# Sharing out the inverse stage's items in front of and behind a W piece, in an FNet and H3 kernel on one core

## The chip, the core and the metric

The kernel runs on one core of a Trainium2 chip. A core has five engines with an instruction queue each: TensorE (PE, matrix products, its weight loads shown as PEld), VectorE (DVE), ScalarE (ACT), GpSimd (POOL) and SyncE (SP, which here only issues transfers). Transfers issued from SP, ACT and POOL share 16 DMA engines. The metric is the device time of one execution in microseconds; three executions of the kernel before are given, and one more was taken by the profiler.

## The reference, cut to what matters

Four residual layers of 2048 rows by 576 columns follow each other: A, B, A, B. A is a Fourier mixing layer, written as products with cosine and sine matrices. B is a long convolution along the rows, per column, with gates.

```python
def _A_ref(x, dft_seq_re, dft_seq_im, dft_hid_re, dft_hid_im):
    a = jnp.einsum("bsd,ed->bse", x, dft_hid_re)
    b = jnp.einsum("bsd,ed->bse", x, dft_hid_im)
    return jnp.einsum("ts,bse->bte", dft_seq_re, a) - jnp.einsum("ts,bse->bte", dft_seq_im, b)

def _B_ref(q, k, v, shift_k, ssm_k, ssm_D):
    k_shift = ...                      # causal convolution of k with 4 taps
    kv = k_shift * v
    kv_f = rfft(pad(kv)); kf_f = rfft(pad(ssm_k))
    y = irfft(kv_f * kf_f)[:, :S, :] + kv * ssm_D
    return q * y

x = A_x
x = x + _A_ref(_layernorm(x), ...)
x = x + _B_ref(_layernorm(x), B_k, B_v, B_shift_k, B_ssm_k, B_ssm_D)
x = x + _A_ref(_layernorm(x), ...)
x = x + _B_ref(_layernorm(x), B_k, B_v, B_shift_k, B_ssm_k, B_ssm_D)
```

The convolution y depends on k, v and the kernels alone, not on x. It is computed once and used by both B layers.

## The kernel before, in words

Two streams of work share the engines. The first is the **layer** stream, the first A layer. It runs 4 row blocks of 512 times 2 parts (cosine, sine) times 16 slices of 128, which makes 128 steps numbered n, 32 to a row block. A step of the layer loads one 128x512 tile of the sequence matrix (SP), splits it into a high and a low part (`split`: one ACT instruction, one DVE instruction, lines 99 and 100), and multiplies: 12 matmuls into the accumulators s_69 to s_72 and 2 into rm, all 512 columns wide. When both parts of a row block are done, its result U must still be multiplied with the hidden matrices W. This is the work of `hidden`: 8 **W pieces** to a row block, each 27 matmuls of 288 columns into one PSUM bank, which a DVE instruction then adds to the residual (line 289). `finish(pending, 1)` emits one W piece. The pieces of a row block are emitted during the next block: one behind each odd step up to n % 32 = 13, and what is left at step 15 of the block. So the pieces of the last group here stand at n = 97, 99, 101, 103, 105, 107, 109 and 111. This text calls them W97 to W111.

The second stream is the **branch**, the convolution, a generator `br` whose every `next` emits a little and returns a cost. From n = 47 on it has two kinds of item. The first 64 are middle items (forward product, product with the kernel's spectrum, inverse product); each ends in a store to the scratch tensor vd, issued from ACT's queue (line 550). The 32 others are **inverse items** (`i2_products`, line 552): a load of one slice of vd from SP (line 580), a split into `mid` by ACT (line 514) and DVE (line 520), four matmuls of 288 columns into two banks, and for each of the banks an ACT copy (line 514) and a DVE addition (line 561) of 64 partitions, and a store to yb from SP (line 562). Ten inverse items stand between middle items, and 22 behind the last one. Those 22 are the six items E10 to E15, which need the first column half of vd, and then F0 to F15, which need the second half. Every F item reads what all of the last 32 middle items stored, so the first F load waits for the last store.

W pieces, middle products and inverse items take their banks from one ring of three (`bank`, tile name bk), in the order in which they are emitted. An inverse item takes two, a W piece one. Buffers for the stores of middle and inverse items come from one ring of four (`vo`).

What paces the branch is a count. `passed` grows by a step's estimated time whenever the layer yields (about STEP = 3.2 for a step) and by PIECE = 3.6 for a W piece, each in estimated microseconds; `spent` is the branch's cost so far, 3.1 for a middle item and 2.0 for an inverse one. As long as `spent < work * passed / total` (line 816), the next item is emitted. In the kernel before this loop stands behind `finish(pending, 1)` and `passed += PIECE`, so that whatever falls due by the step or by the piece is emitted behind the piece. What the branch emits carries an order edge behind the newest residual addition on DVE (`behind(*added, *evac)`). A scheduler then puts the emitted instructions into the engines' queues, and each engine works its queue off in order.

Of the kernel before, what the change touches and what calls it, by code (L numbers as in the profile page):

```python
# [45 lines left out]
I2_LATE = 6  # L46
I2_COST = 2.0
PIECE = 3.6
STEP = 3.2
KP = 4  # L50
H = 2 * P
# [15 lines left out]
def fnet_h3_kernel(ctx: ExitStack, tc: tile.TileContext, x, c_mat, w_re, w_im, k_pad, v, shift_k,  # L67
# [7 lines left out]
    def mm(ps, lhsT, rhs, first, last, more=False):  # L75
        return nc.tensor.matmul(ps, lhsT, rhs, start=first, stop=last, skip_group_check=more).ins  # L76
# [25 lines left out]
    @contextmanager  # L102
    def behind(*instructions):
        with ExitStack() as stack:
            for i in instructions:
                stack.enter_context(tc.issue_after(i))
            yield
# [11 lines left out]
    def region_b(dt, name):  # L119
        return sb.tile([P, 6 * WIDE], dt, tag="rb", name=name)  # L120
# [11 lines left out]
    def lay(t, at, *sizes):  # L132

        for name, words, n in sizes:
            ring.setdefault(name, Ring()).tiles.extend(t[:, at + i * words:at + (i + 1) * words] for i in range(n))
            at += n * words
        assert at <= t.shape[1], (at, t.shape, sizes)
        return at

    def fresh(*names):  # L140
        for name in names:
            ring[name] = Ring()
# [20 lines left out]
    anchor, made, rounded, pows, biased, halved, added, evac, parted, stored = [], [], [], [], [], [], [], [], [], []  # L163
# [51 lines left out]
    def load_c(step):  # L215
        g, tb, k = step
        raw = ring["craw"]()
        anchor.append(load_after(raw, c_mat[g, tb, k]) if anchor else nc.sync.dma_start(raw, c_mat[g, tb, k]).ins)
        c = ring["cs"]()
        t = c[:, :NT], c[:, NT:]  # L220
        with behind(*stored):
            halved[:] = split(t[0], t[1], raw)
        CT[step] = t
# [44 lines left out]
    def evac_r(g, ps):  # L268
        if g == 0:
            U[8] = ut(8)  # L270
        lo, other = (0, REM) if g == 0 else (REM, 0)
        u = U[8][lo:lo + REM]
        tmp = ring["rt"]()[lo:lo + REM]
        nc.scalar.activation(tmp, ps[NC][other:other + REM], AF.Copy)
        nc.vector.tensor_tensor(tmp, tmp, ps[NC][lo:lo + REM], OP.add)  # L275
        evac[:] = split(u[:, 0, :], u[:, 1, :], tmp)

    def hidden(us, tb, jj, xres, done, late=False):
        j = TB * tb + jj
        r = ring["res"]()  # L280
        (load_after if late else nc.sync.dma_start)(r, xres(j))
        for hf in range(2):
            ps = bank()
            cs = slice(hf * HD, (hf + 1) * HD)
            for ch in range(9):
                for n, (a, b) in enumerate(((0, 0), (0, 1), (1, 0))):
                    mm(ps[:, :HD], us[ch][:, a, jj * P:(jj + 1) * P], W[ch][:, b, cs],
                       ch == 0 and n == 0, ch == 8 and n == 2)
            added[:] = [nc.vector.tensor_tensor(r[:, cs], r[:, cs], ps[:, :HD], OP.add).ins]  # L289
            yield  # L290
        done(j, r)

    def finish(pending, pieces):
        while pending and pieces:
            if not isinstance(pending[0], types.GeneratorType):
                pending[0] = hidden(*pending[0])
            if next(pending[0], 0) == 0:
                pending.pop(0)
            else:
                pieces -= 1  # L300

    def layer(get_x, xres, done, pending, blocks=TB):
        steps = [(g, tb, k) for tb in range(blocks) for g in range(2) for k in range(J)]
        for n, (g, tb, k) in enumerate(steps):
            for i in range(2):
                if n == 0 and steps[i] not in CT:
                    load_c(steps[i])
            if n + 2 < len(steps):
                load_c(steps[n + 2])
            for i in range(XLEAD + 1 if blocks == TB else 1):  # L310
                if n + i < J:
                    get_x(n + i)
            if k == 0:
                ps = list(acc4)
                ps.append(psp.tile([P, NT], F32, tag="rm", name="rm"))
            c = CT.pop(steps[n])
            first, last = k == 0, k == J - 1
            while last and g == 0 and pending:
                yield n, None
            for dc in range(NC):  # L320
                xh = X[k][:, dc * P:(dc + 1) * P]
                xl = X[k][:, D + REM + dc * P:D + REM + (dc + 1) * P]
                mm(ps[dc], xh, c[0], first, False)
                mm(ps[dc], xh, c[1], False, False)
                seq[:] = [mm(ps[dc], xl, c[0], False, last)]
                if dc == NC // 2 - 1:
                    yield n, False
                elif blocks == TB and dc < NC - 1 and n >= MID_FROM and not last:
                    yield n, "part"
                if last:  # L330
                    (evac_u if blocks == TB else save_u)(g, ps, dc)
            xr = X[k][:, NC * P:D + REM]
            mm(ps[NC], xr, c[0], first, False)
            seq[:] = [mm(ps[NC], xr, c[1], False, last)]
            if last and blocks < TB:
                store_r(tb, g, ps[NC])
            elif last:
                evac_r(g, ps)
                if g == 1:
                    us = dict(U)  # L340
                    pending.extend([us, tb, jj, xres, done] for jj in range(TB))
            yield n, True
# [423 lines left out]
    br = branch()  # L766
# [21 lines left out]
    spent = passed = 0.0  # L788
    total = (I2_END + 1 - MID_FROM) * STEP + 3 * 2 * TB * PIECE
    work = 64 * 3.1 + 32 * I2_COST  # L790
    for n, whole in layer(get_x0, lambda j: x[:, j, :], done0, pending):
        part = whole == "part"
        if part:
            whole = False
        if (whole or whole is not None and n % J < J - 1) and n <= F1_END and not part:
            at = n if whole else n - 0.5
            at16 = 4 + 2 * F1_16
            want = int(4 + F1_16 * at / 8 if at <= 16 else at16 + (68 - at16) * (at - 16) / (F1_END - 16))
            with behind(made[min(n + 2, J - 1)], *evac):
                while used < want:  # L800
                    next(br)
                    used += 1
        if whole is not None and not part and n >= W_FROM and len(W) < 9:
            with behind(*stored):
                next(wl)
        if whole and n == MID_LOAD:
            with behind(*asked):
                next(br)
        if n >= MID_FROM:
            if whole is not None:  # L810
                share = (5 if whole else 3) if n % J < J - 1 else (8 if whole else 6)
                passed += STEP * share / 14 * BORDER.get(n % J, 1.085)
            if whole is None or whole and n % 2 == 1 and n % (2 * J) < J - 1 and pending:
                finish(pending, 1)
                passed += PIECE
            while spent < work * min(1.0, passed / total):
                with behind(*added, *evac):
                    spent += next(br, work)
        if not whole:
            continue  # L820
        if n >= W_SAVE and n % 2 == 0:
            next(wl, 0)
        m = n - PREP
        if m == 0:
            lay(flts, SC_AT + CRAW * NT + 2 * D, ("xa", D, 2), ("yb", D, 2))
            old = ring["craw"]
            held = [old(), old()]
            fresh("craw")
            lay(flts, SC_AT + CRAW * NT + 6 * D, ("craw", NT, 1))
            ring["craw"].tiles.extend(held)  # L830
            gate = region_b(F32, "gate")
            lay(gate, 0, ("xa", D, 4), ("yb", D, 4), ("xj", D, 2))
        if 0 <= m and n < HOLD:
            advance(m // 2 if m % 2 == 0 and m < 2 * EARLY else None)
# [66 lines left out]
    def store_r(tb, g, ps):  # L901
        lo, other = (0, REM) if g == 0 else (REM, 0)
        t = ring["rt"]()[lo:lo + REM]
        nc.scalar.activation(t, ps[other:other + REM], AF.Copy, scale=1.0 if g == 0 else -1.0)
        nc.vector.tensor_tensor(t, t, ps[lo:lo + REM], OP.add if g == 0 else OP.subtract)
        nc.scalar.dma_start(u_d[tb][8, lo:lo + REM], t)
# [268 lines left out]
```

## Time and profile before

| what | value |
| --- | --- |
| three executions: middle value, lowest | 1182.12 us, 1180.59 us (the third took 4165.63 us) |
| profiled execution, its own time | 1181.27 us |
| profiled execution, span from first to last instruction | 1179.5 us |
| mean granted TensorE clock in it | 0.999 |
| PE, DVE, ACT busy, share of the span | 99%, 74%, 55% |

The profile is of one execution. Its own time is 1.8 us above its span. A busy share is the time in which an engine had an instruction under way; matmuls overlap, so that their busy times do not add up, and a short wait can hide inside a busy stretch. Such a wait shows where the starts of successive rows stand further apart than their matmuls need.

### The profile page before, as it was taken

The numbers are of one execution on the slowest core, as the hardware profiler recorded it, in microseconds if no ns is written. First come the engines' busy times: TensorE is split into PE (matmuls) and PEld (weight loads), VectorE is DVE, ScalarE is ACT, GpSimd is POOL, SyncE is SP. The second block draws the span as 40 slices with busy tenths as digits, with TensorE's granted clock in tenths as the row PEclk, the third lists the DMA queues.
The fourth block names the chain that finished last, engine by engine and source line by source line (L and its number), as shares of the span: only waits on it lengthen the run. The fifth ranks groups of instructions, "written<-read, shape, count | busy, mean of one in ns | idle before, by whom it ended". The sixth has DMA issues, their size and how long they took to land.

```text
span 1179.5 us, 18144 instructions
## 1 busy us (share of the span) xinstructions
PE 1167.0 (99%) x6198; PEld 988.8 (84%) x6198; DVE 867.0 (74%) x1564; ACT 647.6 (55%) x1280; POOL 75.7 (6%) x115
## 2 busy tenths in 40 slices
PE   8999999999999999999999999999999999999997
PEld 6776667988899888888888898888888888889997
DVE  7899983788777778877757766865776777774764
ACT  7865655577766667766645666534444445450210
POOL 2310000000000000001101111000000000001111
PEclk9999999999999999999999999999999999999999
DMA  9879898456656666648956777762762777795621
GB/s 325 297 228 308 263 292 291 156 153 177 215 196 211 198 181 193 192 140 241 286 185 215 249 250 239 241 236 89 252 240 72 233 273 259 263 323 164 201 103 41
DMA packets 147455, 255.67 MB, mean 217 GB/s; under 512 B 16161, under 2 KB 56353, under 8 KB 147362
## 3 DMA queue, kind: packets, MB, share of 16 engines
q1 hardware_dynamic: 111890, 210.17, 55.7%
q10 hardware_dynamic: 28560, 37.91, 9.1%
q0 software_dynamic: 6912, 6.43, 2.4%
q8 instruction: 49, 0.80, 0.3%
q14 instruction: 44, 0.36, 0.1%
HBM read 187.80 MB, written 66.65 MB: 216 GB/s over the span
## 4 chain that ended last, share of the span: by engine, by line
PE 90%; DVE 4%; DMA 3%; ACT 2%; issue 1%; SPq 0%; POOL 0%; DVEq 0%; ACTq 0%
PE s L76 52%; PE bk L76 29%; PE rm L76 6%; PE bf L76 2%; DMA flts<-in_ssm_k 1%; DMA t<-ud 1%; DVE f1f L395 1%; ACT flts L514 1%; DVE mid L520 0%; DVE mats L100 0%; DVE f1f L400 0%; DMA early<-in_x 0%; DVE u L100 0%; DMA vd<-flts 0%; DMA flts<-vd 0%
## 5 line engine op out<-in xcount | busy, mean ns | idle before, releaser
L76 PE MATMUL s<-mats 128*128 128x512 f32 x2102 | 549.4, 395 | 4.3 <-ACT mats L197 2.3
L76 PEld LDWEIGHTS s<-mats 128*128 128x128 f32 x2102 | 382.0, 188 | 84.6 <-issue 10.7
L100 DVE TENSOR_TENSOR mats<-flts,mats 128x512 fp32r<-128x512 f32 x206 | 140.9, 688 | 50.4 <-ACT mats L99 46.1
L99 ACT ACTIVATE mats<-flts 128x512 fp32r<-128x512 f32 x206 | 128.1, 627 | 78.9 <-PE bk L76 34.3
L514 ACT ACTIVATE flts<-bk 128x288 f32<-128x288 f32 (+1 forms) x192 | 78.5, 409 | 101.6 <-PE bk L76 83.4
L76 PE MATMUL bk<-mid 128*128 128x288 f32 x704 | 131.1, 301 | 0.3
L76 PEld LDWEIGHTS bk<-mid 128*128 128x128 f32 x704 | 110.7, 188 | 22.0 <-ACT flts L514 5.1
L76 PE MATMUL bk<-w,u 128*128 128x288 f32 x864 | 119.9, 295 | 0.1
L76 PEld LDWEIGHTS bk<-w,u 128*128 128x128 f32 x864 | 117.5, 188 | 2.7 <-ACT flts L514 0.8
L520 DVE TENSOR_TENSOR mid<-flts,mid 128x576 fp32r<-128x576 f32 (+1 forms) x149 | 92.2, 624 | 5.9 <-ACT mid L514 4.2
L76 PE MATMUL rm<-mats 128*128 128x512 f32 x304 | 94.6, 391 | 0.3 <-DVE flts L275 0.3
L514 ACT ACTIVATE mid<-flts 128x576 fp32r<-128x576 f32 (+1 forms) x148 | 79.5, 574 | 1.8 <-DVE flts L561 0.7
L289 DVE TENSOR_TENSOR flts<-flts,bk 128x288 f32<-128x288 f32 x48 | 21.8, 453 | 72.6 <-PE bk L76 72.6
L76 PE MATMUL bk<-mats 128*128 128x288 f32 (+1 forms) x376 | 67.8, 317 | 0.0
L76 PEld LDWEIGHTS rm<-mats 128*128 128x128 f32 x304 | 56.9, 188 | 12.9 <-PE s L76 0.7
L453 ACT ACTIVATE flts<-bf 128x384 f32<-128x384 f32 (+1 forms) x104 | 43.2, 462 | 43.9 <-PE bf L76 42.5
L76 PE MATMUL s<-t,mats 128*128 128x512 f32 x264 | 65.2, 390 | 0.1
L186 POOL TENSOR_TENSOR flts<-flts 128x1 f32<-128x1 f32 x34 | 28.0, 824 | 518.2 <-DVE flts L185 515.8
L76 PE MATMUL bk<-mats,t 128*128 128x288 f32 (+1 forms) x368 | 59.3, 303 | 0.0
L514 ACT ACTIVATE flts<-flts 64x288 f32<-64x288 f32 x128 | 56.7, 443 | 3.9
L76 PEld LDWEIGHTS s<-t,mats 128*128 128x128 f32 x264 | 49.4, 188 | 10.9 <-DVE t L100 0.7
L76 PEld LDWEIGHTS bk<-mats 128*128 128x128 f32 x376 | 55.5, 188 | 3.4
(152 smaller groups left out, 1495.6 us busy)
## 6 DMA issues: line engine op xcount, KB each, us to landing
flts<-in_c_mat SPq DMA_DIRECT2D x148, 256.0 KB, 3.5
ph<-in_c_mat SPq DMA_DIRECT2D x54, 512.0 KB, 4.1
flts<-in_c_mat SPq DMA_DIRECT2D x30, 512.0 KB, 5.4
flts<-td SPq DMA_DIRECT2D x53, 288.0 KB, 3.0
td<-flts ACTq DMA_DIRECT2D x36, 384.0 KB, 4.8
vd<-flts ACTq DMA_DIRECT2D x64, 144.0 KB, 3.0
flts<-vd SPq DMA_DIRECT2D x32, 288.0 KB, 4.4
ud<-ph ACTq DMA_DIRECT2D x12, 512.0 KB, 6.5
```

Source lines behind the costliest of these rows:

```text
L76: return nc.tensor.matmul(ps, lhsT, rhs, start=first, stop=last, skip_group_check=more).ins
L99: a = nc.scalar.activation(h, src, AF.Copy).ins
L100: return a, nc.vector.tensor_tensor(l, src, h.bitcast(F32), OP.subtract).ins
L186: pows.append(nc.gpsimd.tensor_tensor(rs, ve, mhalf, OP.pow).ins)
L289: added[:] = [nc.vector.tensor_tensor(r[:, cs], r[:, cs], ps[:, :HD], OP.add).ins]
L395: nc.vector.tensor_tensor(out_t[:, n], k, wt[3 - t][:, n], OP.mult)
L453: stored[:] = [nc.scalar.activation(so[:, i, :], ps[i], AF.Copy).ins]
L514: last_act.append(nc.scalar.activation(*args, **kw).ins)
L520: nc.vector.tensor_tensor(l, src, h.bitcast(F32), OP.subtract)
```

## The change

The counting of a W piece is cut in two for the last part of the branch. The pacing loop becomes a function, `keep_up`, that is called twice around a W piece: once in front of it and once behind it. As long as the branch has not spent the 64 middle items and ten inverse items (64 * 3.1 + 10 * 2.0 = 218.4), nothing of the piece is counted in front; the first call still emits what the step itself has made due. From then on half of PIECE, 1.8, is counted in front of the piece, and the other half behind it. The sum of the counts is what it was.

```diff
--- before.py
+++ after.py
@@ -46,6 +46,8 @@
 I2_LATE = 6
 I2_COST = 2.0
 PIECE = 3.6
+BEFORE = PIECE / 2
+I2_SPREAD = 10
 STEP = 3.2
 KP = 4
 H = 2 * P
@@ -788,6 +790,13 @@
     spent = passed = 0.0
     total = (I2_END + 1 - MID_FROM) * STEP + 3 * 2 * TB * PIECE
     work = 64 * 3.1 + 32 * I2_COST
+
+    def keep_up():
+        nonlocal spent
+        while spent < work * min(1.0, passed / total):
+            with behind(*added, *evac):
+                spent += next(br, work)
+
     for n, whole in layer(get_x0, lambda j: x[:, j, :], done0, pending):
         part = whole == "part"
         if part:
@@ -811,11 +820,12 @@
                 share = (5 if whole else 3) if n % J < J - 1 else (8 if whole else 6)
                 passed += STEP * share / 14 * BORDER.get(n % J, 1.085)
             if whole is None or whole and n % 2 == 1 and n % (2 * J) < J - 1 and pending:
+                ahead = BEFORE if spent >= 64 * 3.1 + I2_SPREAD * I2_COST else 0.0
+                passed += ahead
+                keep_up()
                 finish(pending, 1)
-                passed += PIECE
-            while spent < work * min(1.0, passed / total):
-                with behind(*added, *evac):
-                    spent += next(br, work)
+                passed += PIECE - ahead
+            keep_up()
         if not whole:
             continue
         if n >= W_SAVE and n % 2 == 0:
```

The built programs hold the same matmuls, copies, additions and transfers. What differs is their order from the W pieces of the third row block (n = 65 to 79) on. The names in the following rows: `bk<-w,u` is a W piece (27 matmuls), `bk<-mid` are matmuls of middle or inverse items (four to an inverse item), s_69 to s_72 and rm are the layer's. The changed file has two lines more above these, so that line 76 of before is line 78 of the change, and lines 514 and 550 are 516 and 552.

The first place is PE's queue around W105, before. The piece is followed by three inverse items close together: four matmuls, two and two, two and two.

```order
L76 MATMUL bk<-w,u 128x288 x27
L76 MATMUL bk<-mid 128x288 x4
L76 MATMUL s_69<-mats 128x512
L76 MATMUL bk<-mid 128x288 x2
L76 MATMUL s_69<-mats 128x512 x2
L76 MATMUL bk<-mid 128x288 x2
L76 MATMUL s_70<-mats 128x512 x3
L76 MATMUL bk<-mid 128x288 x2
L76 MATMUL s_71<-mats 128x512
L76 MATMUL bk<-mid 128x288 x2
L76 MATMUL s_71<-mats 128x512 x2
L76 MATMUL s_72<-mats 128x512 x3
```

The same place of the change.

```order
L78 MATMUL bk<-mid 128x288 x4
L78 MATMUL bk<-w,u 128x288 x27
L78 MATMUL bk<-mid 128x288 x4
L78 MATMUL s_69<-mats 128x512 x3
L78 MATMUL s_70<-mats 128x512 x3
L78 MATMUL bk<-mid 128x288 x4
L78 MATMUL s_71<-mats 128x512 x3
L78 MATMUL s_72<-mats 128x512 x3
L78 MATMUL rm<-mats 128x512 x2
```

One inverse item has moved to the front of the piece, and the next one behind the piece stands after six matmuls of the layer, in one block. Of the 22 items, 1, 4, 5, 5, 4 and 3 stood in front of W101, between W101 and W103, and so on to behind W109; now it is 2, 5, 4, 5, 5 and 1. At W97 and W99, and at two pieces of the block before, three matmuls of a middle item have moved from behind the piece to its front.

The second place is ACT's queue at the end of the middle items, before. `flts<-bk 128x288` is the copy of the last middle product, `vd_81<-flts` its store; the pairs of 64x288 are copies of inverse items, here of E10 and then of E11, and `mid<-flts` is a split for a later item.

```order
L514 ACTIVATE flts<-bk 128x288
L514 ACTIVATE flts<-bk 64x288 x2
L514 ACTIVATE mid<-flts 128x576
L550 DMA vd_81<-flts 128x288
L514 ACTIVATE flts<-bk 64x288 x2
L514 ACTIVATE mid<-flts 128x576
```

The same place of the change.

```order
L516 ACTIVATE flts<-bk 128x288
L516 ACTIVATE flts<-bk 64x288 x2
L516 ACTIVATE mid<-flts 128x576
L516 ACTIVATE flts<-bk 64x288 x2
L516 ACTIVATE mid<-flts 128x576
L552 DMA vd_81<-flts 128x288
L516 ACTIVATE flts<-bk 64x288 x2
```

The store of the last middle item has moved behind the copies of E11 and the split for E13. On SP the load for F0, which waits for that store, has likewise moved behind the two stores of E11.

The third place is PE's queue around W103, before. Here E14 is followed by a step, then comes W103, then E15 (four matmuls), the first two of F0, and behind two of the layer the other two of F0 with one of F1.

```order
L76 MATMUL s_69<-mats 128x512 x3
L76 MATMUL bk<-mid 128x288 x4
L76 MATMUL s_70<-mats 128x512 x3
L76 MATMUL s_71<-mats 128x512 x3
L76 MATMUL s_72<-mats 128x512 x3
L76 MATMUL rm<-mats 128x512 x2
L76 MATMUL bk<-w,u 128x288 x27
L76 MATMUL bk<-mid 128x288 x4
L76 MATMUL s_69<-mats 128x512
L76 MATMUL bk<-mid 128x288 x2
L76 MATMUL s_69<-mats 128x512 x2
L76 MATMUL bk<-mid 128x288 x3
```

The same place of the change. Again it begins with the step that E14 stands in.

```order
L78 MATMUL s_69<-mats 128x512 x3
L78 MATMUL bk<-mid 128x288 x4
L78 MATMUL s_70<-mats 128x512 x3
L78 MATMUL s_71<-mats 128x512 x3
L78 MATMUL s_72<-mats 128x512 x3
L78 MATMUL rm<-mats 128x512 x2
L78 MATMUL bk<-mid 128x288 x6
L78 MATMUL s_69<-mats 128x512 x3
L78 MATMUL s_70<-mats 128x512
L78 MATMUL bk<-mid 128x288 x2
L78 MATMUL s_70<-mats 128x512
L78 MATMUL bk<-w,u 128x288 x27
```

E15 and F0 have both moved to the front of W103.

## The prediction

> **What bounds the kernel now.** I read the page's busy line first, then the slices and the chain of work that ended last.
>
> ```profile
> PE 1167.0 (99%) x6198; PEld 988.8 (84%) x6198; DVE 867.0 (74%) x1564; ACT 647.6 (55%) x1280; POOL 75.7 (6%) x115
> PEclk9999999999999999999999999999999999999999
> PE 90%; DVE 4%; DMA 3%; ACT 2%; issue 1%; SPq 0%; POOL 0%; DVEq 0%; ACTq 0%
> ```
>
> PE is under way for 99% of the span at the full granted clock, and the chain is PE for 90%. The change adds and removes no instruction, so it can only win or lose time in which PE stands still between two matmuls. Busy shares hide such time. So I went to the timeline of PE, from W105 to the end of the step behind it (start, duration, what, count).
>
> ```profile
> 559.30 1.54 PE L76 MATMUL s<-mats 128*128 128x512 f32 x6
> 560.68 0.79 PE L76 MATMUL bk<-mid 128*128 128x288 f32 x4
> 561.31 1.54 PE L76 MATMUL s<-mats 128*128 128x512 f32 x6
> 562.69 0.61 PE L76 MATMUL rm<-mats 128*128 128x512 f32 x2
> 563.14 3.71 PE L76 MATMUL bk<-w,u 128*128 128x288 f32 x27
> 566.70 0.69 PE L76 MATMUL bk<-mid 128*128 128x288 f32 x4
> ...
> 569.21 0.73 PE L76 MATMUL bk<-mid 128*128 128x288 f32 x2
> 569.79 0.40 PE L76 MATMUL s<-mats 128*128 128x512 f32 x1
> ...
> 571.57 0.62 PE L76 MATMUL rm<-mats 128*128 128x512 f32 x2
> ...
> 572.55 2.24 PE L76 MATMUL s<-mats 128*128 128x512 f32 x9
> 574.63 0.69 PE L76 MATMUL bk<-mid 128*128 128x288 f32 x4
> 575.15 0.85 PE L76 MATMUL s<-mats 128*128 128x512 f32 x3
> ```
>
> Undisturbed matmuls give a pitch: six wide ones from 561.31 to 562.69 are 0.230 us each, 27 narrow ones from 563.14 to 566.70 are 0.132 us each. Behind the piece, from 566.70 to 571.57, stand 12 narrow and 12 wide matmuls (the order's rows of W105). They need 1.58 + 2.76 = 4.34 us and took 4.87: **0.53 us of standing still** at one W piece. At 569.21 one pair alone took 0.58 instead of 0.26. An inverse item takes two banks of three and each bank is emptied by an ACT copy and a DVE addition, so the third item in a row has no bank yet. The other rows show what distance costs: behind six wide matmuls an item takes 0.63 (560.68 to 561.31) instead of 0.53, so 0.10 is lost; behind nine it takes 0.52, and nothing is lost.
>
> For the whole stage I take the groups of PE from W97 to the start of W111, and the pieces' rows.
>
> ```profile
> 508.34 3.71 PE L76 MATMUL bk<-w,u 128*128 128x288 f32 x27
> 597.39 3.77 PE L76 MATMUL bk<-w,u 128*128 128x288 f32 x27
> L76 PE MATMUL s<-mats 128*128 128x512 f32 x156 | 43.3, 392 | 0.0
> L76 PE MATMUL bk<-mid 128*128 128x288 f32 x145 | 28.7, 307 | 0.2
> L76 PE MATMUL bk<-w,u 128*128 128x288 f32 x189 | 26.2, 295 | 0.0
> L76 PE MATMUL rm<-mats 128*128 128x512 f32 x27 | 8.6, 390 | 0.0
> ```
>
> The stretch is 89.05 us long. One of the 27 rm is the end of the step before, so 182 wide matmuls at 0.230 and 334 narrow ones at 0.132 need 41.86 + 44.09 = 85.95. PE stood still for **3.1 us** in all, 0.26% of the execution. That is the most that this change can win here, and it is far below the 2% (24 us) that a measurement of this kernel can tell from no change.
>
> **The change, part by part.** First, the inverse items around the W pieces. An item in front of a piece and one behind it share no waiting: the piece's 27 matmuls last 3.56 us, in which ACT and DVE empty the first item's banks. The nine wide matmuls of 572.55 to 574.63, 2.08 us, were cover enough for that; without the piece's cover a neighbour would lose the 0.3 of the pair at 569.21. Behind the piece the second item now follows after six wide matmuls, not one. I go through the 22 items of the changed order and count the wide matmuls between neighbours without a piece between them. Seven gaps have six or fewer: E12 to E13, E13 to E14, E15 to F0, F2 to F3, F5 to F6, F8 to F9, F13 to F14. The rest have eight to eleven. At 0.10 each the seven cost 0.7 us, the others nothing.
>
> Second, what does not change: the end of the middle items in front of W101 has the same rows in both orders.
>
> ```profile
> 536.28 1.26 PE L76 MATMUL bk<-mid 128*128 128x288 f32 x7
> 537.37 0.86 PE L76 MATMUL s<-mats 128*128 128x512 f32 x3
> ```
>
> Seven narrow matmuls took 1.09 there instead of 0.92, so 0.17 was lost. For this and the like losses from W97 to W101 I estimate three times that, 0.5 of the 3.1 us, and another 0.2 for the rounding of the pitches; both stay.
>
> Third, three matmuls of a middle item in front of a piece instead of behind, four times. The trace shows no such place in front of a piece. Behind the piece these three stood as a fourth group after one wide matmul; in front they follow a full step. I price either place by the 0.10 of a short gap. The bounds are 0.4 won and 0.4 lost; I take 0, since in both places the neighbours hide them.
>
> Fourth, the moved queues. The load of F0 on SP waits for the last middle store on ACT's queue. These are the rows before: ACT's timeline, SP's, DVE's, who SP waited for, and the time to landing of, in turn, the E13 load (issued 536.0), the last store (538.0) and the F0 load (545.0).
>
> ```profile
> 538.01 0.33 ACTq L550 DMA_DIRECT2D vd<-flts  x1
> 538.73 0.69 ACT L514 ACTIVATE mid<-flts 128x576 fp32r<-128x576 f32 x1
> 548.56 0.69 ACT L514 ACTIVATE mid<-flts 128x576 fp32r<-128x576 f32 x1 [0.33 <-DMA flts<-vd]
> 545.04 0.56 SPq L169 DMA_DIRECT2D flts<-vd  x1
> 549.63 0.76 DVE L520 TENSOR_TENSOR mid<-flts,mid 128x576 fp32r<-128x576 f32 x1
> SPq L169 <- DMA vd<-flts: 5.0, 2, 4.6
> DMA to landing us min/median/max: 4.5/4.5/4.5
> DMA to landing us min/median/max: 6.9/6.9/6.9
> DMA to landing us min/median/max: 3.4/3.4/3.4
> 538.07 3.79 PE L76 MATMUL bk<-w,u 128*128 128x288 f32 x27
> 554.22 0.50 PE L76 MATMUL bk<-mid 128*128 128x288 f32 x2
> ```
>
> Before, the store went out at 538.01 and landed at 544.9; SP had waited 4.6 us and issued the load at 545.04; it landed at 548.4, ACT and DVE had split it at 550.39, and PE came to F0 at 554.22, so 3.8 us were to spare. With the change PE comes to F0 earlier: from 538.07 on stand E11, W101, E12 to E15 (47 narrow, 6.2 us) and 24 wide matmuls (5.5 us), which makes 549.8. And the store stands behind the copies of E11, which end PE's work on E11 at about 539.2, and behind the split for E13, whose data landed at 536.0 + 4.5 = 540.5. The row at 538.01 shows that a store can go out ahead of a split that stands in front of it (538.73), where that split waits for nothing. No row shows it passing one that waits. So the store goes out between 538.0 and 540.5. How long it takes:
>
> ```profile
> vd<-flts ACTq DMA_DIRECT2D x64, 144.0 KB, 3.0
> 541.00:543.00 2.00, 2.00 (x15) 1.84 (x14) 0.86 (x2) 0.81 (x2) 0.32 (x1) 1.00 1.08 327
> 543.00:545.00 2.00, 1.95 (x10) 1.27 (x8) 1.72 (x4) 1.91 (x4) 0.74 (x2) 1.00 0.47 120
> ```
>
> The median of such stores is 3.0, this one took 6.9, with the DMA engines full until 543 (share 1.08) and half free behind it (0.47). Bounds for F0's data: issue 538.0 with 3.0 gives a landing at 541.0, long in time; issue 540.5 with 6.9 gives 547.4, then 0.1 and 3.4 for the load and 1.8 for the split, 552.7, which is 2.9 us late. I take issue 540.5 and 4 us, nearer to the median since the engines empty in between: landing 544.5, data at 549.8, and 0.2 for its uncertainty. Queued behind the waiting load on SP are E12's stores and the next loads, and behind a late split on ACT the copies of E15; all wait for the same landing, so they add nothing to the 2.9.
>
> Here a rule of the Trainium skill bears. Its page Perfetto Trace Analysis, section Per-instruction lifecycle, says that an ACT instruction is pushed into a wait queue and waits for its semaphores there, and that the sequencer then decodes the next. By that rule the store would not be held by E11's copies and would still go out at 538.0; with the landing at 544.9 as before, F0 would be 0.6 us late instead of 0.2, and the late case of 2.9 would fall away. No row here shows a store passing an instruction that waits.
>
> **The sum.** 3.1 now; 0.7 + 0.5 + 0.2 + 0.2 = 1.6 later. The gain is 1.5 us. From the profiled execution's 1181.27 that gives **1179.8**; this execution lies 0.85 below the middle one of the three (1182.12) and 0.7 above the lowest (1180.59).
>
> **The rivals.** First, the late F0 (slower): one wait takes the place of the many. Its price is up to 2.9 instead of 0.2, so 1179.8 + 2.7 = 1182.5. It decides from the point where the store lands later than 546.0: then F0 is 1.5 us or more late and the gain is gone. For it speaks that the only F0 chain in the trace took 6.9; against it that the engines were half free from 543 on. Chance 0.2.
>
> Second, the short waits come back in other places. DVE works in order, and a layer split in front of an item's additions would delay its bank; the loss of 0.10 at 560.68 shows that six wide matmuls are not always enough. Were each of the seven gaps to cost the 0.3 that the worst pair lost at 569.21, they would cost 2.1, and the time would be 1181.2. Against it speaks that an item between two pieces now has one close neighbour at most. Chance 0.2.
>
> Third, the items move, but PE does not stand still less, since the places that lose the time are others than I think: 1181.3. That the change does nothing to the order is excluded by the rows of the order; that it does nothing to the time has the chance 0.08.
>
> Fourth, F0 comes so late that the clock falls. PEclk is full in every slice, so no row prices it; if 3.4 us of matmuls ran at half pace behind the late F0, 1.7 us would be lost on top: 1184.2. Chance 0.02. The Trainium skill's page TensorE: Matmul & The Clock Gate, Part 1, gives such a rule: after an idle window of about 3.4 us the clock is half. A wait of 2.9 does not fill it, and no stretch of this trace shows it.
>
> **How the numbers follow.** The forecast has 0.5: 1179.0 to 1180.6. The range reaches down to all of the 3.1 less 0.5 that stays, and further 0.6 for how executions differ (the given ones lie 1.5 apart), 1178.0; and up to the late F0, 1182.5, with 0.7 for the same, 1183.2. The cases beyond it hold less than 0.1. No case reaches 24 us, so within 2% has 0.97, slower 0.02, faster 0.01.
>
> **What the profile would show.** Right: from W101 to W111 the starts of PE's rows leave less than 1.6 us beside the pitches, each item behind a piece takes 0.53, and the pair that took 0.58 is gone. Right in the fourth part: the last store goes out on ACT at about 540, ACT's split of F0 at 548 or so, and PE loses less than half a microsecond in front of F0. Wrong: PE has one long gap in front of F0, with ACT's split waiting for the load of vd; or the gaps of six wide matmuls lose 0.3 each. The forecast is also wrong if the stretches ahead of W97 or behind W111, in which next to nothing is moved, differ by more than half a microsecond.

## The result, and the profile after

| | before | change |
| --- | --- | --- |
| middle of 22 executions | 1180.73 us | 1179.17 us |
| profiled execution, its own time | 1181.27 us | 1178.67 us |
| profiled execution, span | 1179.5 us | 1176.4 us |
| PE standing still from W97 to W111 | 3.1 us | 1.1 us |

The ratio of the change to before is 0.9986, with a 95% interval of 0.998 to 0.9991. The change is faster by 1.6 us, 0.14%; by 2% it is the same. One execution of before that took 4165.63 us is left out of the comparison.

These are the page's busy line, the granted clock and the chain of the change.

```profile
PE 1164.9 (99%) x6198; PEld 989.8 (84%) x6198; DVE 868.2 (74%) x1564; ACT 647.9 (55%) x1280; POOL 75.5 (6%) x115
PEclk9999999999999999999999999999999999999999
PE 94%; DVE 3%; DMA 1%; ACT 1%; issue 1%; SPq 0%; POOL 0%; DVEq 0%; ACTq 0%
```

The counts of all engines are those of before, the clock is full, and PE is still 99% busy. Nothing here tells why the time fell. The groups of PE from W97 to the start of W111 and the two pieces' rows do (each timeline was cut at the edge of a window, hence the small counts).

```profile
L78 PE MATMUL s<-mats 128*128 128x512 f32 x156 | 41.5, 393 | 0.0
L78 PE MATMUL bk<-w,u 128*128 128x288 f32 x189 | 26.2, 294 | 0.0
L78 PE MATMUL bk<-mid 128*128 128x288 f32 x144 | 25.6, 298 | 0.0
L78 PE MATMUL rm<-mats 128*128 128x512 f32 x26 | 8.2, 392 | 0.0
```

```profile
508.42 0.43 PE L78 MATMUL bk<-w,u 128*128 128x288 f32 x2
595.05 1.23 PE L78 MATMUL bk<-w,u 128*128 128x288 f32 x8
```

The stretch is 86.63 us. Two of the 144 narrow matmuls started ahead of it, so 182 wide and 331 narrow ones need 41.86 + 43.69 = 85.55 us at the pitches of the prediction, and 1.1 us is left. It was 3.1. (Three narrow matmuls of the stretch, 0.4 us, now stand in front of W97.) PE around W105, in the timeline of the change:

```profile
561.61 0.69 PE L78 MATMUL bk<-mid 128*128 128x288 f32 x4
562.13 3.71 PE L78 MATMUL bk<-w,u 128*128 128x288 f32 x27
565.68 0.69 PE L78 MATMUL bk<-mid 128*128 128x288 f32 x4
566.21 1.55 PE L78 MATMUL s<-mats 128*128 128x512 f32 x6
567.60 0.69 PE L78 MATMUL bk<-mid 128*128 128x288 f32 x4
568.12 1.55 PE L78 MATMUL s<-mats 128*128 128x512 f32 x6
```

Every item takes its 0.52 to 0.53 us, the one in front of the piece (561.61 to 562.13), the one behind it (565.68 to 566.21), and the one after six wide matmuls (567.60 to 568.12). The pair that had taken 0.58 is gone.

By pieces, in the same arithmetic, the standing still in us between the starts of neighbouring W pieces:

| kernel | W97-99 | 99-101 | 101-103 | 103-105 | 105-107 | 107-109 | 109-111 | sum |
| --- | --- | --- | --- | --- | --- | --- | --- | --- |
| before | 0.17 | 0.58 | 0.59 | 0.64 | 0.51 | 0.12 | 0.49 | 3.1 |
| change | 0.0 | 0.37 | 0.34 | 0.07 | 0.0 | 0.35 | 0.0 | 1.1 |
| change, second profile | 0.0 | 0.38 | 1.58 | 0.04 | 0.0 | 0.35 | 0.0 | 2.3 |

### The profile page after: what moved, and what is told of

It is laid out like the page before. It is cut to its first block, busy times and chain, and to the rows that moved or that the text cites. A ratio compares the mean times of both kernels' runs of the same rounds, so it can differ in the third digit from the quotient of the medians.

```text
span 1176.4 us, 18139 instructions
## 1 busy us (share of the span) xinstructions
PE 1164.9 (99%) x6198; PEld 989.8 (84%) x6198; DVE 868.2 (74%) x1564; ACT 647.9 (55%) x1280; POOL 75.5 (6%) x115
## 4 chain that ended last, share of the span: by engine, by line
PE 94%; DVE 3%; DMA 1%; ACT 1%; issue 1%; SPq 0%; POOL 0%; DVEq 0%; ACTq 0%
PE s L78 55%; PE bk L78 30%; PE rm L78 6%; PE bf L78 2%; DVE f1f L397 1%; DMA early<-in_x 0%; ACT flts L516 0%; DVE f1f L402 0%; DVE mats L102 0%; DMA td<-flts 0%; DMA vd<-flts 0%; DVE f1r L102 0%; DVE u L102 0%; DVE flts L534 0%; ACT u L101 0%
## 5 line engine op out<-in xcount | busy, mean ns | idle before, releaser
L78 PE MATMUL bk<-mid 128*128 128x288 f32 x704 | 128.0, 299 | 0.1
```

## The experiments

The standing still can be read to about 0.1 us in a profile, but a profile is one execution. The times have intervals of about 1 us to either side, so they tell a gain of 1.6 us from none, and not much finer. Both are given. Where the text below says what a kernel won or lost at a place, that is read from its one profile. Ratios are to the kernel before, with 95% intervals. Each comparison had its own executions of before beside it; their middle values were 1181.09 (the first four), 1181.0 (without the additions, and the first with the store on SP), 1180.84 (splits three ahead) and 1180.77 us (the last two).

**The change once more.** No edit.

> The changed kernel once more. Standing still of PE from the start of W97 to the start of W111 (stretch less 0.230 us per wide and 0.132 us per narrow matmul) was 3.1 us before and 1.1 us in the first profile of the change. Theory (the gain is bank waits beside the W pieces): 0.9 to 1.3 us again, and the time 1.2 to 2.4 us under the kernel before. Rival (the gain lies in stretches far from the change, since the two profiles' spans differ by 3.1 us and the stage accounts for 2.0): the stage is not reproducible, or the span lies 3 us under the one before again with the excess in the same far stretches.

Measured: 1179.52 us, ratio 0.9987 (0.9977 to 0.9998), so the gain repeats. The stage did not: 2.3 us of standing still, all of the difference between W101 and W103 (1.58 for 0.34). Everywhere else the two profiles of the change agree within 0.04 us. The timeline of this execution, ACT and PE:

```profile
539.04 0.33 ACTq L552 DMA_DIRECT2D vd<-flts  x1
545.81 0.83 ACT L516 ACTIVATE flts<-bk 64x288 f32<-64x288 f32 x2 [1.39 <-PE s L78]
545.63 0.43 PE L78 MATMUL bk<-mid 128*128 128x288 f32 x2
546.76 0.53 PE L78 MATMUL bk<-mid 128*128 128x288 f32 x2 [0.70 <-DVE flts L563]
549.68 0.81 PE L78 MATMUL bk<-mid 128*128 128x288 f32 x5
550.70 0.40 PE L78 MATMUL bk<-mid 128*128 128x288 f32 x1 [0.20 <-DVE mid L522]
```

The time to landing of the last middle store in it:

```profile
DMA to landing us min/median/max: 6.7/6.7/6.7
```

The store went out at 539.04 and landed 6.7 us later, at 545.7. At 545.81 ACT began E13's copies, after 1.39 us of standing idle, though PE, which the row names, had long done E13: E13's buffer is the one that the last middle store reads, as the ring of four has it. So E14 lost 0.97 us at 545.63 to 547.13, waiting for a bank (DVE, line 563), and F0, whose load waited for the same landing, 0.46 more at 549.68 (a split, DVE line 522). Two things hang on this store. That E13 waits for the buffer shows by name in another profile, that of the change without the additions (below), where the store went out at 540.49 and took 5.5 us:

```profile
546.12 0.84 ACT L516 ACTIVATE flts<-bk 64x288 f32<-64x288 f32 x2 [0.94 <-DMA vd<-flts]
```

The expectation had been that a fifth buffer takes away E14's wait. The kernel with five buffers gave no result, so that stays untried.

**Nothing counted in front.**

```diff
-BEFORE = PIECE / 2
+BEFORE = 0.0
```

> Nothing of the piece is counted in front (BEFORE = 0); the call in front of the piece stays and emits what the step made due. By the order, one item stands in front of W103 and of W109; W101, W105 and W107 have their three items close behind as before. Theory: those three keep what they lost, about 0.5 us each, so the stage stands still 2.0 to 2.5 us, and the time is 0.6 to 1.1 us under before. Rival (the call in front alone does it): the stage stands still 1.1 us, time as the change.

Measured: 1179.46 us, ratio 0.9984 (0.9975 to 0.9992); 1.5 us of standing still. By pieces 0.0, 0.23, 0.59, 0.06, 0.51, 0.12, 0.02: W101 and W105, with three items close behind, keep what they lost before (0.59 and 0.51), and W103 and W109, which now have an item in front, lose nothing. That is the theory piece by piece. The size was less: 1.5 instead of the 2.0 expected at least, since W107 never lost much, and since F0 stands behind W103 here and waits for nothing. In the time this kernel is as good as the change, more than the 0.6 to 1.1 us that were expected. So half of the edit, the call in front of the piece, earns most of the gain (1.6 of the 2.0 us of standing still); the half of PIECE in front repairs W105 and part of W101, where the early F0 and its wait for a split come in.

**The call in front only when something is counted there.**

```diff
                 passed += ahead
-                keep_up()
+                if ahead:
+                    keep_up()
```

> The call in front of the piece is made only once half of the piece is counted there, so the four groups of three middle matmuls stand behind their pieces again, and from W101 on the order is that of the change. Theory: 1.1 to 1.5 us of standing still from W97 to W111, time within 0.5 us of the change. Rival (the moved middle matmuls earn a good part): 1.8 us or more, time 0.8 us or more over the change.

Measured: 1179.40 us, ratio 0.9983 (0.9974 to 0.9991); 1.8 us, by pieces 0.16, 0.70, 0.55, 0.08, 0.0, 0.36, 0.0. With the groups of three middle matmuls behind W97 and W99 again, those two stretches lose 0.86 for the 0.34 to 0.39 of the change. So the moved middle matmuls earn about 0.5 us here, and 0.3 more in the block before (0.63 us between its pieces, 0.63 less the change's 0.30 to 0.33). In the time of the kernel this does not show. The 1.8 fits neither expectation well: 0.4 of it is F0's wait at W103.

**All of the piece in front.**

```diff
-BEFORE = PIECE / 2
+BEFORE = PIECE
```

> The whole piece is counted in front (BEFORE = PIECE). By the order two to three items stand close together in front of each piece instead of behind it. Theory (items close together wait for banks, on whichever side): 2.0 to 3.0 us of standing still, time within 1 us of before. Rival (what counts is only that the place behind the piece is free): 1.1 us, time as the change.

Measured: 1181.87 us, ratio 1.0004 (0.9996 to 1.0012); 3.4 us of standing still. The gain is gone: items close together wait in front of a piece as they did behind it. The largest loss, 1.91 us ahead of W101, has a cause of its own. PE's timeline:

```profile
538.21 0.86 PE L78 MATMUL s<-mats 128*128 128x512 f32 x3
540.37 0.37 PE L78 MATMUL bk<-mid 128*128 128x288 f32 x1 [1.30 <-DMA mid<-in_i2c]
```

E12, the third item in front of W101, came before its constants had landed: their transfer, issued at 535.47, landed at 540.24. That is a third kind of wait, and it comes from standing early.

**Without the additions, before and change.** The inverse items of both kernels leave out the two DVE additions that join the product with the low part of the constants, so y lacks these corrections.

```diff
                 act(yo[main], ps[i][main, :HD], AF.Copy)
-                nc.vector.tensor_tensor(yo[main], ps[i][corr, :HD], yo[main], OP.add)
```

> The kernel before, and the inverse items leave out their two additions (line 561), so that half of each item's sum is missing from y, and a bank is empty after one ACT copy. Theory (banks not yet emptied hold PE beside the W pieces): the stage from W97 to W111 stands still 1.0 to 1.8 us instead of 3.1, the third item behind a piece no longer loses 0.3. Rival (what holds PE there is the data of the items, not the banks): 2.5 us or more as before.

> The changed kernel with the same additions left out. Theory: 0.5 to 1.2 us apart from the wait for the last middle store (which moved between 0.1 and 1.4 us in the profiles so far), so that the two orders differ by 0.7 us or less where they differed by 2.0. Rival: they differ by 1.5 us or more.

Measured: the kernel before without them 1181.44 us, ratio 1.0007 (0.9998 to 1.0016), 2.7 us of standing still; the changed one 1181.47 us, 0.9997 (0.9987 to 1.0006), 2.0 us, of which 1.14 lies between W101 and W103, with the late store (out at 540.49, F0's load at 546.09). With that stretch left out of both, the two orders differ by 1.4 us, and by 1.8 with the additions. The theory had asked for 0.7 or less, so the additions are a small part of what the difference hangs on, and my theory of the banks fails in this form. The times do not decide it: without the additions the two orders are level (1181.44 and 1181.47), but the executions of the changed one spread from 1178.73 to 1183.63, and the profiled one is the longest of them. Who PE's weight loads waited for behind W105 says why the additions matter little; first before, then before without the additions (waited for: us in total, times, longest).

```profile
PEld bk L76 <- DVE mid L520: 0.4, 1, 0.4
PEld bk L76 <- DVE flts L561: 0.2, 1, 0.2
```

```profile
PEld bk L76 <- DVE mid L520: 0.4, 1, 0.4
```

The 0.4 us at the third item, in front of its second weight load, is not a bank. It is the low half of that item's split (line 520). The chain in the kernel before:

```profile
567.16 0.84 ACT L514 ACTIVATE flts<-bk 64x288 f32<-64x288 f32 x2 [3.29 <-PE bk L76]
568.02 0.69 ACT L514 ACTIVATE mid<-flts 128x576 fp32r<-128x576 f32 x1
568.74 0.76 DVE L520 TENSOR_TENSOR mid<-flts,mid 128x576 fp32r<-128x576 f32 x1 [0.20 <-ACT mid L514]
569.55 0.19 PEld L76 LDWEIGHTS bk<-mid 128*128 128x128 f32 x1 [0.38 <-DVE mid L520]
```

A split is emitted two items ahead, so the third item's split stands behind the first item's copies on ACT, which begin when the piece ends. The first item's additions on DVE (567.60 to 568.54) were over 0.20 us before the split's low half could begin, so leaving them out could not shorten this chain.

**Splits three items ahead, before and change.** Behind the last middle item, a fourth df buffer, and:

```diff
-            split_feed(i + 2)
+            split_feed(i + split_ahead)      # 2, and 3 behind the last middle item
```

> The kernel before, and behind the last middle item each inverse item's split into mid is made three items ahead instead of two (a fourth df buffer). Leaving out the additions had not shortened the waits (2.7 us of standing still for 3.1), and PE's weight loads of the items waited 1.7 us for splits (ACT and DVE mid) and 1.6 us for banks from W97 to W111. New theory (the third item behind a piece waits for its split, which comes behind the copies of the item two before): 1.2 to 2.1 us of standing still, time 0.8 to 1.6 us under before. Rival (banks alone, as the prediction had it): 2.7 us or more, time as before.

> The changed kernel with splits three ahead. New theory: the change and the earlier split take away the same waits, so that from W103 to W111 nothing more than 0.3 us is to be won, 0.0 to 0.3 us of the 0.4 left there; the last store goes out earlier than 539.0 since E13's split no longer stands in front of it on ACT. F0's split now stands in front of E15's copies, so a late landing may hold E15 as well. Stage 0.8 to 2.0 us, time within 0.6 us of the change. Rival (independent gains): stage under 0.6 us, and time 2.5 us or more under before.

Measured: before with it 1180.66 us, ratio 1.0001 (0.9992 to 1.0009), 2.8 us of standing still. This theory fails too, by itself. The waits behind W105 in it:

```profile
PEld bk L76 <- DVE flts L561: 0.5, 1, 0.5
```

The split is no longer waited for, and a bank is, for as long: 0.5 instead of 0.4 and 0.2. The change with it took 1179.62 us, ratio 0.999 (0.9981 to 0.9999), 1.7 us; from W103 to W111 it has 0.4, as the change has. The store went out at 536.73 there, since E13's split no longer stood in front of it, and still 0.98 us was lost from W101 to W103.

**Both at once, in the kernel before.** Without the additions and with splits three ahead.

> The kernel before with both edits at once: the inverse items leave out their additions, and their splits are made three items ahead. One edit alone left 2.7 and 2.8 us of standing still of 3.1. New theory (three items close behind a piece wait for whatever of two chains is still behind: the second item's banks or the third item's split, which end near together; DVE has 0.94 + 0.76 us of work per item and ACT 0.84 + 0.69): with both shortened the third item no longer waits at W103, W105 and W109, and the stage stands still 1.0 to 1.8 us. Rival (the waits have a third cause that neither edit touches, the rate of ACT's 1.53 us per item): 2.4 us or more.

Measured: 1180.48 us, ratio 0.9999 (0.999 to 1.0008); 1.8 us of standing still, by pieces 0.16, 0.57, 0.20, 0.67, 0.04, 0.10, 0.05. Behind W105 what either edit alone had left (0.38 and 0.49) is gone. Behind W101 0.53 and 0.59 have become 0.20, behind W109 0.45 and 0.23 have become 0.05. PE behind W105 in this kernel:

```profile
565.85 0.69 PE L76 MATMUL bk<-mid 128*128 128x288 f32 x4
566.38 0.39 PE L76 MATMUL s<-mats 128*128 128x512 f32 x1
566.61 0.76 PE L76 MATMUL bk<-mid 128*128 128x288 f32 x4
567.20 1.32 PE L76 MATMUL s<-mats 128*128 128x512 f32 x5
568.36 0.69 PE L76 MATMUL bk<-mid 128*128 128x288 f32 x4
568.88 1.53 PE L76 MATMUL s<-mats 128*128 128x512 f32 x6
```

The second item loses 0.06 and the third nothing (568.36 to 568.88). So two chains held the third item, its split and its bank, that end near each other; taking away one shows the other. Behind W103 the expectation fails: the third item there, F1, still loses 0.57 us (554.40 to 555.50), waiting for a bank of F0 that ACT copied only at 554.66, behind a split of 0.69. In the time, the 1.3 us that the profile shows won do not appear: the middle values differ by 0.3, and the interval ends at 1.2. The mechanism is shown in the profile, its worth in the time is not.

**The last store from SP, in the change, twice; and with splits three ahead.**

```diff
-            nc.scalar.dma_start(v_d[hf][...], vo)
+            (nc.sync if (hf, qg) == (1, 31) else nc.scalar).dma_start(v_d[hf][...], vo)
```

> The changed kernel, and the last middle store alone is issued from SP's queue instead of ACT's, where it stood behind E11's copies and E13's split. Theory (the store is held on ACT): it goes out at 537.0 to 538.0 instead of 539.0 to 539.9, and PE loses 0.4 us or less from W101 to W103 (0.34 and 1.58 in the two profiles of the change). Rival (the landing is set by full DMA engines up to 543, whenever the store goes out): the landing is at 543.5 or later all the same, and the loss from W101 to W103 stays between 0.3 and 1.6 us.

> The changed kernel with the last middle store issued from SP, once more. Theory: the store goes out before 538.0 and PE loses 0.4 us or less from W101 to W103 again, stage 0.9 to 1.2 us, time 1.2 to 2.4 us under before. Rival (the good W101 to W103 of the first such profile was luck of the landing): 0.6 us or more there.

> The changed kernel with splits three ahead and the last middle store issued from SP. Theory: the store lands by 542.5, no wait for F0, 0.5 to 1.0 us of standing still from W97 to W111, time 1.7 to 2.6 us under before. Rival (one of the two edits costs as much as it wins): 1.2 us or more, time within 1.5 us of before.

Measured: 1179.12 us, ratio 0.9987 (0.9978 to 0.9995), and again 1179.27 us, 0.9986 (0.9977 to 0.9996). Both profiles have 1.0 us of standing still, 0.29 and 0.28 between W101 and W103. SP's timeline of the first, and the store's time to landing:

```profile
536.93 0.33 SPq L552 DMA_DIRECT2D vd<-flts  x1
541.93 0.56 SPq L171 DMA_DIRECT2D flts<-vd  x1
```

```profile
DMA to landing us min/median/max: 4.9/4.9/4.9
```

The store goes out 2.1 to 3.0 us earlier than in the change, lands 4.9 us later (5.4 in the second), and F0's load follows at 541.93 instead of 544.27 or 545.78. What is left there is the gap from E15 to F0: F0's second pair waits for a bank (0.29 us, 549.12 to 550.59). With splits three ahead as well it is 1179.69 us, 0.9992 (0.9983 to 1.0), and 2.0 us: the store went out at 536.05, and W101 to W103 lost 0.98, at banks (1.6 us of waits for line 563). That splits three ahead cost something where the items are spread is what the profile of this kernel and of the change with them (0.98 too) agree on. Why is not shown. In both kernels with the store on SP a split stands in front of E13's additions on DVE; with splits three ahead E14 also comes sooner behind W101 (6.0 us after its start, 6.9 without), and meets the wait.

No kernel here beats the change in the time by more than the interval. The change with the store on SP has the least standing still, and it is steady in two profiles.

## Why the prediction was right, and where it was not

The forecast was 1179.8 us and a gain of 1.5 us; measured were 1179.17 and 1.6. The bound that it began with held: no kernel of either order won more than the 3.1 us that PE stood still.

The nearness of 1.5 and 1.6 is in part luck. In the stage itself the first profile of the change won 2.0 us and the second 0.8, and the block before won another 0.3 that the prediction had at nothing.

**The W pieces.** That an item in front of the piece and one behind share no waiting is what the profile shows, at W103, W105 and W109, and nothing counted in front proves it piece by piece. But the step "each bank is emptied by an ACT copy and a DVE addition, so the third item in a row has no bank yet" was half of it. Of the waits of that item's weight loads 0.4 us was its split, the other 0.2 a bank. Additions left out kept the wait for the split, splits made earlier made the wait for the bank longer; both together took them away. The piece covers both chains, which is why the step's conclusion stood.

**The price of the short gaps.** Seven gaps at 0.10 made 0.7. Items six wide matmuls apart in the change lost 0.0 (567.60 to 568.12). Two gaps of the list, E15 to F0 and F13 to F14, where the second item follows the first at once and then stands in front of a piece, lost about 0.3 each, and the rest of their stretches little (0.34 and 0.35 in all). The sum, 0.7, came out for the wrong gaps, which is luck. The 0.2 for a late F0 came on top in the prediction; in the runs it did not. F0's late split took 0.24 of what the gap from E15 to F0 lost in the change, but with the store on SP, where F0 was on time, the gap lost 0.29 all the same, at F0's bank.

**What stays in front of W101.** I kept 0.5 there and 0.2 for rounding. 0.34 stayed.

**The moved middle matmuls.** I took 0 from bounds of 0.4 to either side. By the profiles of the change and of the kernel without these moves they won about 0.5 from W97 to W101 and 0.3 in the block before; the upper end was nearer, and too low.

**The moved store.** This step held closely. The timeline of the change, and the store's time to landing:

```profile
539.86 0.69 ACT L516 ACTIVATE mid<-flts 128x576 fp32r<-128x576 f32 x1 [0.44 <-DMA flts<-vd]
539.92 0.35 ACTq L552 DMA_DIRECT2D vd<-flts  x1
544.27 1.22 SPq L171 DMA_DIRECT2D flts<-vd  x2
547.85 0.69 ACT L516 ACTIVATE mid<-flts 128x576 fp32r<-128x576 f32 x1 [0.54 <-DMA flts<-vd]
548.59 1.19 PE L78 MATMUL bk<-mid 128*128 128x288 f32 x6
549.62 1.09 PE L78 MATMUL s<-mats 128*128 128x512 f32 x4
```

```profile
DMA to landing us min/median/max: 4.3/4.3/4.3
```

The store went out at 539.92, 0.06 us after E13's split began, which had waited for its data; forecast was 540.5. The store goes with the landing of those data, not with the split: in the five profiles with the store in this place (two of the change, and one each of the call in front only when something is counted there, of all of the piece in front, and of the change without additions) it went out 0.03 to 0.09 us after E13's load had landed, and in the second profile of the change, at 539.04, ahead of the split, which began at 539.50. It took 4.3 us, forecast 4. E15 and F0's first pair took 1.03 us instead of 0.79, so 0.24 was lost, forecast 0.2. The rule of the Trainium skill's page Perfetto Trace Analysis (section Per-instruction lifecycle), that the sequencer goes on while an instruction waits in the queue, would have let the store go at 537.1, when the last middle copy was done. It did not.

**The late F0.** The second profile of the change is this rival: with the landing after 6.7 us PE lost 1.24 us more than in the first between W101 and W103. The prediction's chain gives 545.7 + 0.1 + 3.4 + 1.8 = 551.0 for F0's data, 1.2 late. What it got wrong is "so they add nothing": E13's copies hung on the same store through its buffer, and most of the loss (0.97 of it) was E14's bank, not F0. The point from which the gain would be gone, a landing later than 546.0, was just missed. A long landing is not a rare case: the last store took 4.3 us and 6.7 in the change, and 6.9 in before.

**The sign that spoke against it.** The prediction called itself wrong if the stretches ahead of W97 or behind W111 differed by more than half a microsecond. Ahead of W97 they differ by 0.1, behind W111 by 0.7 (582.1 us before, 581.4 in both profiles of the change). The sign was set too tight: the two profiles of the change with the store on SP, one and the same kernel, differ there by 1.3 us (582.0 and 583.4). One such place is the layer's waits for splits from 1015 to 1045 us, where PE's weight loads waited 0.7 us in before, 0.2 in the change, and 2.1 in the second profile with the store on SP. The two profiled executions of before and change differ by 2.6 us, more than the 1.6 of the middle values; 2.0 is the stage and 0.3 the block before.

## What to carry to other kernels

When an engine is 99% busy, take its undisturbed pitch from two starts and count the matmuls of a stretch: what is left is all that a new order can win, and here that was 0.26% before anything else was asked. A long piece of matmuls that needs the other engines little is cover; small items that need copies, additions and splits go on both sides of it, not in a heap on one side. Where a wait in such a heap is taken away and the time stays, look which second chain ends at the same place before giving the theory up; and when items are moved forward, follow the slowest transfer they depend on, with the whole range of its landing times, and everything that reuses its buffer.

## What was not expected

- The same 144 KB store, issued at nearly the same place, took 4.3, 4.9, 5.4, 6.7 and 6.9 us to land in five profiles, and 4.3 to 6.8 in eight others; the median of such stores is 3.0 us. The DMA engines were full around it in the profile of before (share 1.08 to 1.09 from 539 to 543).
- On ACT a store stands behind a split that still waits for its data, though not behind a copy or a split that is only queued: 538.01 in before, ahead of a split that began at 538.73, and 539.92 in the change, within 0.1 us of the landing of the data that the split in front of it waited for.
- Leaving out 44 additions of 0.46 us on DVE, 20 us of its work, in the 90 us where the branch's items are densest, did not make the kernel measurably faster (1.0007, 0.9998 to 1.0016), nor the changed one (0.9997, 0.9987 to 1.0006). The chain through ACT's copies and split held PE all the same.
